# A reordered opening: whole quarters of w_in, an earlier w_out request, two convolution taps on TensorE

## The chip, the cores and the metric

The kernel runs on one core of a Trainium2 chip. The metric is the device time of one execution in microseconds (us), lower is better. A verdict of faster or slower needs 2%, which here is 13.8 us. Each timed execution also gives its span, from the first to the last instruction, which is 1.7 us shorter than its time. A profile is one execution, and its own time is listed with it.

## The reference

A causal convolution over the sequence, with seven softmaxed weights for each of 8 heads, feeds an MLP with the activation h times sigmoid(beta h).

```python
w = exp(weight - max); w = w / (sum(w) + 1e-9)              # (8 heads, 7 taps)
out[b, s, h, g] = sum over k of w[h, k] * x_pad[b, s + k, h, g]
x = out.reshape(32768, 192)
h = x @ w_in                                                # (192, 2048)
g = h * (1 / (1 + exp(-beta * h)))
y = g @ w_out                                               # (2048, 192)
```

x is (8, 4096, 192) in float32.

## The kernel before

The tokens go through in 32 chunks (two times 512 tokens each). A chunk has 16 units `u`, each for 128 of the 2048 hidden columns:

- **TensorE** makes the hidden values of the unit (6 matmuls, two at a time) and, for earlier units, products with w_out ("pairs").
- **ScalarE** applies Silu to the unit: one instruction of 128x1024 elements.
- **VectorE** makes the convolution of a coming chunk: a product and six multiply-adds ("taps"), and other small work.

From chunk 1 on this is a steady pipeline. The change touches the opening only: the loads, chunk 0 (where the convolution of two of three channel groups is made by TensorE with diagonal matrices) and chunk 1's preparation, which is made while chunk 0's 16 units run.

```python
    load_x(x0, 0)                 # chunk 0's tokens, chunk 1's tokens
    load_x(x1, TOK)
    load_w_out(0)                 # four quarters of w_out, SyncE's queue, in this order
    load_w_out(1)
    load(2)                       # chunk 2's tokens
    load_w_out(2)
    load_w_out(3)
    load(3)
    # ... cut ...
    load_w_in(0, FW // 2)         # w_in on GpSimd's queue: first quarter in two halves
    # ... cut ...
    fill(5)                       # filler matmuls on zeros
    # ... cut: product for the softmax weights, filler, casts of x0 ...
    load_w_in(FW // 2, FW)
    for i in range(1, NW):
        load_w_in(i * FW, (i + 1) * FW)
    # ... cut: transposes of chunk 0's tokens with filler between them, the diagonals ...
    new_ct(0)
    for c in range(NG - 1):       # groups 0 and 1 of chunk 0: seven diagonal matmuls each
        pv = in_b() if c else psum_h.tile([128, 2, TOK], FP32, name="ph")
        for k in range(K):
            diag_tap(k, xt0[:, c], pv[:, 0, :])
        for b in range(2):
            cast_rows(nc.scalar.copy, x1b, x1, 2 * c + b)
        nc.scalar.copy(cts[0][:, c, :], pv[:, 0, :])
    # ... cut ...
    for k in range(K):            # group 2 of chunk 0: seven taps on VectorE
        o = HALO - PAD + k
        tap(cts[0][:, NG - 1, :], xt0[:, NG - 1, o : o + TOK].bitcast(FP32), k)
    nc.vector.reciprocal(beta_r, beta)
    scale_w_out(0)                # w_out / beta, one quarter, on VectorE
    # ... cut ...
    CONV1 = {4: (0, 2), 5: (2, 4), 6: (4, K)}   # unit: diagonal taps of chunk 1's group 0
    # ... cut ...
    first_work = {                # VectorE's work in chunk 0, by unit; None is one tap of chunk 1
        4: [None],
        5: [lambda: scale_w_out(1), None],
        7: [None, conv1_evac],    # conv1_evac copies chunk 1's diagonal sums out of PSUM
        8: [None],
        9: [lambda: scale_w_out(2)],
        10: [None, lambda: rows_of(2)],         # casts and transposes of chunk 2
        11: [None],
        12: [lambda: scale_w_out(3), None],
    }
```

In these traces VectorE takes its list in the order of the program: in the kernel before, the scaling of the third w_out quarter waits 0.44 us until 25.05, and the tap behind it starts at 25.93.

Of the kernel before, what the change touches and what calls it, by code (L numbers as in the profile page):

```python
# [17 lines left out]
def kernel(  # L18
# [147 lines left out]

    load_x(x0, 0)
    load_x(x1, TOK)
    load_w_out(0)
    load_w_out(1)  # L170
    load(2)
    load_w_out(2)
    load_w_out(3)
    load(3)

    zeros = setup.tile([128, TOK], BF16)
    nc.vector.memset(zeros, 0.0)
    warm = setup.tile([H, 1], FP32)
    nc.vector.memset(warm, 0.0)  # L179
    nc.scalar.activation(warm, warm, AF.Exp)  # L180

    sel = setup.tile([H, 2, DG], FP32)
# [20 lines left out]
    ident = setup.tile([128, 128], FP32)  # L203
    make_identity(nc, ident)

    def load_w_in(c0, c1):
        for r in range(2):
            nc.gpsimd.dma_start(  # L208
                out=w_in_s[r * DG : (r + 1) * DG, :, c0:c1], in_=w_in_v[:, :, c0:c1]
            )  # L210

    load_w_in(0, FW // 2)

    nmax = setup.tile([H, 1], FP32)
    nc.vector.reduce_max(nmax, cw8, axis=mybir.AxisListType.X, negate=True)
# [38 lines left out]
    nc.tensor.matmul(  # L254
        pw, sel.rearrange("i h p -> i (h p)"), e8, start=True, stop=True
    )
    fill(1, 256)
    nc.tensor.transpose(pb, beta_q, ident[0:NF, 0:NF])
    nc.scalar.copy(beta, pb)
    for b in range(2):  # L260
        cast_rows(nc.vector.tensor_copy, x0b, x0, b)
    nc.vector.reciprocal(rn, pw[:, K : K + 1])
    nc.vector.tensor_scalar_mul(cw, pw[:, 0:K], rn)
    for b in range(2, NB):
        cast_rows(nc.vector.tensor_copy, x0b, x0, b)

    hold = setup.tile([1, 1], BF16)
    nc.gpsimd.tensor_copy(hold, x0b[0:1, 0, 0, 0, 0:1])
    load_w_in(FW // 2, FW)
    for i in range(1, NW):  # L270
        load_w_in(i * FW, (i + 1) * FW)

    diag = setup.tile([128, K, 128], FP32R)
    xt0 = setup.tile([128, NG, HALO + TOK], FP32R)
    nc.vector.memset(xt0[:, :, 0:HALO].bitcast(FP32), 0.0)
    xt1 = setup.tile([128, HALO + TOK], FP32R)
    cts = {}

    def new_ct(s):
        cts[s] = ct_pool.tile([128, NG, TOK], BF16, name="ct")  # L280

    def diag_tap(k, xt, pv, rows=slice(0, 128)):
        o = HALO - PAD + k
        nc.tensor.matmul(  # L284
            pv,
            diag[rows, k, :],
            xt[rows, o : o + TOK],
            start=(k == 0),
            stop=(k == K - 1),
        )  # L290

# [4 lines left out]
    for b in range(NB):  # L296
        pt = pts[b % 2][:, b // 2, 0 : NG * BLK].rearrange("p (c q) -> p c q", c=NG)
        transposes(pt, x0b, b)
        nc.scalar.copy(tokens(xt0, b), pt)  # L299
        fill(1, 256 if b % 2 else 128)  # L300
    fill(1, 256)
    nc.vector.tensor_tensor(
        diag,
        ident.unsqueeze(1).to_broadcast((128, K, 128)),
        cw.unsqueeze(2).to_broadcast((128, K, 128)),
        ALU.mult,
    )

    def scale_w_out(i):
        fcs = slice(i * NQ, (i + 1) * NQ)  # L310
# [9 lines left out]
    for c in range(NG - 1):  # L320
        pv = in_b() if c else psum_h.tile([128, 2, TOK], FP32, name="ph")
        for k in range(K):
            diag_tap(k, xt0[:, c], pv[:, 0, :])
        for b in range(2):
            cast_rows(nc.scalar.copy, x1b, x1, 2 * c + b)
        nc.scalar.copy(cts[0][:, c, :], pv[:, 0, :])

    def tap(dst, src, k):
        scalar = cw[:, k : k + 1]
# [4 lines left out]
                out=dst, in0=src, scalar=scalar, in1=dst, op0=ALU.mult, op1=ALU.add  # L334
            )

    for k in range(K):
        o = HALO - PAD + k
        tap(cts[0][:, NG - 1, :], xt0[:, NG - 1, o : o + TOK].bitcast(FP32), k)
    nc.vector.reciprocal(beta_r, beta)  # L340
    scale_w_out(0)

# [26 lines left out]
        nc.vector.tensor_copy(xt1[:, HALO - PAD :], xt[:, 0, HALO - PAD :])  # L369


    CONV1 = {4: (0, 2), 5: (2, 4), 6: (4, K)}
    conv1_ps = []

    def conv1(u):
# [131 lines left out]
    def rows_of(ch):  # L507
        for h in range(2):
            cast(ch, h)
        xpose(ch)  # L510


    first_work = {
        4: [None],
        5: [lambda: scale_w_out(1), None],
        7: [None, conv1_evac],
        8: [None],
        9: [lambda: scale_w_out(2)],
        10: [None, lambda: rows_of(2)],
        11: [None],  # L520
        12: [lambda: scale_w_out(3), None],
    }

    queue = deque()
    for s in range(N_ST):
        jobs_of(s)
        for u in range(NF):
            if s > 0 or u > 1:
                hidden(s, u)
            elif u == 0:  # L530
                phs = [hidden(0, fc, [0]) for fc in range(2)]
                for j in range(1, NG):
                    for fc in range(2):
                        hidden(0, fc, [j], phs[fc])
                second()
            if s > 0:
                output(s, u, 8 if s < N_ST - 1 else 7, "ab")
            elif u > 7:
                output(s, u, 5, "ab")
            elif u == 3 or u == 7:  # L540
                output(s, u, 5, "a")
            if s == 0:
                if u in CONV1:
                    conv1(u)
                if u == min(CONV1):
                    queue.extend(conv_ops(1, 1))
                for work in first_work.get(u, []):
                    (work or queue.popleft())()
            else:
                if u % 2 and queue:  # L550
                    queue.popleft()()

                if u == 0 and s + 3 < N_CH:
                    load(s + 3)
                if u < 2 and s + 2 < N_CH:
                    cast(s + 2, u)
                if u == 1 and s + 2 < N_CH:
                    xpose(s + 2)
            if u == 12 and s + 2 < N_CH:
                queue.extend(conv_ops(s + 2, 0))  # L560
# [32 lines left out]
```

## Time and profile before

| | before |
|---|---|
| time, median of 4 executions | 692.34 us (692.31 to 693.17) |
| profiled execution | 693.01 us, span 691.3 |
| TensorE busy | 684.0 us |
| first Silu | 14.11 us |
| last tap of chunk 1 ends | 31.73 us |
| first and second Silu of chunk 1 | 32.92 and 34.39 us |

The profile page of the kernel before. The first line is the span; the second is busy time and share of each engine; the third is the DMA queue of w_in (packets, MB, share of time).

```profile
span 691.3 us, 24335 instructions
...
PE 684.0 (99%) x11310; PEld 497.2 (72%) x11310; DVE 527.2 (76%) x466; ACT 579.1 (84%) x531; POOL 8.1 (1%) x20
...
q0 software_dynamic: 2080, 1.57, 1.5%
...
```

TensorE is busy 99%. In the steady state a unit takes 1.307 us (0.65 for the hidden matmuls, 0.65 for eight pairs), and every Silu of 1.11 us is followed by a wait of 0.19 us for TensorE. Nothing in the opening can change that. It can only let it start earlier. Two lines of TensorE's timeline of the kernel before (start, duration, engine and line, operation, count, idle time before it and what ended it):

```profile
...
7.51 3.29 PE L284 MATMUL ph<-xt,diag 128*128 128x512 f32 x7 [0.16 <-ACT xt L299]
10.64 1.79 PE L284 MATMUL pb<-xt,diag 128*128 128x512 f32 x7
...
```

The first seven diagonal matmuls take 3.1 us until the next group starts, the same seven of the next group 1.7 us. Until about 10.6 us these matmuls start 0.43 us apart, then 0.23, and the trace's clock record starts with full clock at 10.60 us. I read the lower clock as half: the record has no entry before 10.60, and the only other value in it is 0.5, at the very end. (The page's clock row shows 9, that is 90% or more, for the whole span all the same.) The Trainium skill, "TensorE: Matmul & The Clock Gate", Part 1, says that full clock is granted after a free-running window of about 3.4 us of activity. The trace agrees with a lower clock first, and with a change in one step (0.43 to 0.23 us within one matmul).

ScalarE's timeline of the kernel before, from the first Silu to the second Silu of chunk 1:

```profile
...
14.11 4.14 ACT L417 ACTIVATE g<-ph,beta 128x1024 bf16<-128x1024 f32 x4 [0.97 <-PE ph L409]
18.96 3.37 ACT L417 ACTIVATE g<-ph,beta 128x1024 bf16<-128x1024 f32 x3 [0.71 <-PE ph L409]
22.57 4.29 ACT L417 ACTIVATE g<-ph,beta 128x1024 bf16<-128x1024 f32 x4 [0.23 <-PE ph L409]
27.34 4.29 ACT L417 ACTIVATE g<-ph,beta 128x1024 bf16<-128x1024 f32 x4 [0.47 <-PE ph L409]
31.86 2.17 ACT L417 ACTIVATE g<-ph,beta 128x1024 bf16<-128x1024 f32 x2 [0.23 <-PE ph L409]
34.39 1.11 ACT L417 ACTIVATE g<-ph,beta 128x1024 bf16<-128x1024 f32 x1 [0.35 <-PE ph L409]
...
```

The 16 Silus of chunk 0 would take 17.2 us in a row. They take 18.8, because ScalarE stands idle 0.71, 0.23, 0.47 and 0.23 us, each time for hidden values that TensorE made late. Why they were late at the end is told by the chain that ended last, in order of time (start, duration, what). It is followed back from the end of the kernel, here from 10 to 36 us:

```profile
...
7.79 17.24 DMA w_out_raw<-in_moe_w_out_dram
...
25.05 0.96 DVE w_out_s L311
26.01 1.20 DVE ct L333
27.20 1.20 DVE xb L106 x2
...
28.48 1.19 DVE ct L333
29.66 0.88 DVE w_out_s L311
...
30.59 0.34 PE pa L442 x4
...
```

The chain starts with a transfer: the third quarter of w_out lands at 25.03 us. VectorE then scales it at once (25.05) and has a fixed queue behind it: a tap, chunk 2's casts, a tap, the fourth quarter, for whose scaling TensorE waits at 30.59.

### The profile page before, as it was taken

How to read it: one execution, taken by the hardware profiler on the slowest of the kernel's cores; microseconds unless marked ns; L12 is line 12 of the kernel's file. 1: busy time of each engine (PE TensorE's matmuls, PEld its weight loads, DVE VectorE, ACT ScalarE, POOL GpSimd, SP SyncE). 2: the span in 40 equal slices, each digit the busy share in tenths (PEclk: the TensorE clock that was granted, in tenths of full speed). 3: DMA queues.
4: the chain of work that ended last, by engine and by line, in shares of the span. 5: the costliest groups of instructions: out<-in, count | busy, mean ns of one | idle time of the engine just before them, and what ended most of it. 6: DMA issues, size and time to landing. Idle time of an engine off the chain costs nothing.

```text
span 691.3 us, 24335 instructions
## 1 busy us (share of the span) xinstructions
PE 684.0 (99%) x11310; PEld 497.2 (72%) x11310; DVE 527.2 (76%) x466; ACT 579.1 (84%) x531; POOL 8.1 (1%) x20
## 2 busy tenths in 40 slices
PE   8999999999999999999999999999999999999997
PEld 5677777777777777777777777777777777777776
DVE  7888877797777797777887777887777977777712
ACT  6888888888888888888888888888888888888893
POOL 4000000000000000000000000000000000000000
PEclk9999999999999999999999999999999999999999
DMA  9754332343332343332444332443323433322111
GB/s 221 169 117 116 90 103 65 92 116 104 99 103 58 104 116 104 93 94 62 113 116 94 102 81 74 116 116 93 102 61 95 116 105 99 102 55 60 48 37 59
DMA packets 121861, 66.86 MB, mean 97 GB/s; under 512 B 53264, under 2 KB 121760, under 8 KB 121760
## 3 DMA queue, kind: packets, MB, share of 16 engines
q1 hardware_dynamic: 119632, 63.73, 34.7%
q0 software_dynamic: 2080, 1.57, 1.5%
q8 instruction: 88, 1.44, 0.9%
q14 instruction: 13, 0.11, 0.1%
q10 hardware_dynamic: 48, 0.01, 0.0%
HBM read 29.89 MB, written 25.17 MB: 80 GB/s over the span
## 4 chain that ended last, share of the span: by engine, by line
PE 95%; DMA 2%; SPq 1%; DVE 1%; ACT 0%; issue 0%
PE ph L409 47%; PE pa L442 24%; PE pb L442 24%; DMA w_out_raw<-in_moe_w_out_dram 2%; SPq L95 1%; DVE ct L333 0%; SPq L160 0%; DVE w_out_s L311 0%; DVE xb L106 0%; ACT g L417 0%; SPq L148 0%; ACT osb L458 0%; DVE xt L121 0%
## 5 line engine op out<-in xcount | busy, mean ns | idle before, releaser
L417 ACT ACTIVATE g<-ph,beta 128x1024 bf16<-128x1024 f32 x512 | 569.7, 1114 | 97.3 <-PE ph L409 91.4
L442 PEld LDWEIGHTS <-g 64*128 64x128 bf16 x8160 | 353.6, 94 | 121.1 <-issue 1.3
L409 PE MATMUL ph<-ct,w_in_s 64*128 64x512 bf16 x3072 | 416.8, 376 | 1.5 <-ACT g L417 0.9
L333 DVE SCALAR_TENSOR_TENSOR ct<-xt,cw,ct 128x1536 bf16<-128x1536 bf16 (+2 forms) x192 | 338.3, 1762 | 2.5
L442 PE MATMUL pa<-w_out_s,g 64*128 64x192 bf16 x4112 | 238.9, 243 | 0.9 <-ACT g L417 0.5
L442 PE MATMUL pb<-w_out_s,g 64*128 64x192 bf16 (+1 forms) x4048 | 224.9, 243 | 0.0
L409 PEld LDWEIGHTS <-w_in_s 64*128 64x128 bf16 x3072 | 143.0, 94 | 64.0 <-DMA w_in_s<-in_moe_w_in_dram 1.6
L460 DVE TENSOR_REDUCE osb<-pa 128x384 f32<-128x768 f32 x64 | 61.3, 958 | 121.5 <-PE pa L442 121.2
L460 DVE TENSOR_REDUCE osb<-pb 128x384 f32<-128x768 f32 x63 | 60.3, 958 | 28.8 <-PE pb L442 28.8
L106 DVE CAST xb<-xf 128x768 bf16<-128x768 f32 x60 | 40.6, 679 | 0.0
L331 DVE TENSOR_SCALAR ct<-xt,cw 128x1536 bf16<-128x1536 bf16 (+2 forms) x32 | 31.2, 974 | 0.2 <-ACT xt L299 0.2
L208 POOL DMA_DIRECT2D w_in_s<-in_moe_w_in_dram x10 | 6.5, 654 | 2.4 <-DMA w_in_s<-in_moe_w_in_dram 2.4
L458 ACT COPY osb<-pb 128x192 f32<-128x192 f32 x1 | 0.3, 319 | 6.7 <-PE pb L442 6.7
L226 PE MATMUL ph<-zeros 128*128 128x512 bf16 (+2 forms) x11 | 4.4, 493 | 1.3 <-DVE warm L179 1.3
L284 PE MATMUL pb<-xt,diag 64*128 64x512 f32 (+1 forms) x21 | 5.1, 445 | 0.0
L121 DVE COPY xt<-xt 128x18 bf16<-128x18 bf16 x27 | 4.3, 160 | 0.0
L311 DVE TENSOR_TENSOR w_out_s<-w_out_raw,beta_r 128x768 bf16<-128x768 f32 x4 | 3.8, 954 | 0.5 <-DMA w_out_raw<-in_moe_w_out_dram 0.4
L284 PEld LDWEIGHTS pb<-xt,diag 64*128 64x128 f32 (+1 forms) x21 | 3.4, 194 | 0.5
L284 PE MATMUL ph<-xt,diag 128*128 128x512 f32 x7 | 3.3, 643 | 0.2 <-ACT xt L299 0.2
L231 ACT CAST x1b<-x 128x384 bf16<-128x384 f32 x4 | 2.7, 717 | 0.7 <-DMA x<-in_x_dram 0.7
L284 PEld LDWEIGHTS ph<-xt,diag 128*128 128x128 f32 x7 | 2.1, 324 | 1.1 <-ACT xt L299 0.6
L226 PEld LDWEIGHTS <-zeros 128*128 128x128 bf16 x11 | 1.4, 140 | 2.1 <-DVE warm L179 1.3
(48 smaller groups left out, 23.2 us busy)
## 6 DMA issues: line engine op xcount, KB each, us to landing
out_dram<-osb SPq DMA_DIRECT2D x127, 192.0 KB, 2.1
xf<-in_x_dram SPq DMA_DIRECT2D x60, 384.0 KB, 4.3
xt<-xb SPq DMA_TRANSPOSE x120, 3.0
x<-in_x_dram SPq DMA_DIRECT2D x4, 384.0 KB, 5.1
w_out_raw<-in_moe_w_out_dram SPq DMA_DIRECT2D x4, 384.0 KB, 13.4
w_in_s<-in_moe_w_in_dram POOLq DMA_DIRECT2D x6, 192.0 KB, 12.2
w_in_s<-in_moe_w_in_dram POOLq DMA_DIRECT2D x4, 96.0 KB, 8.8
out_dram<-osb SPq DMA_DIRECT2D x2, 96.0 KB, 1.6
```

What stands on the lines that cost most here:

```text
L95: nc.sync.dma_start(out=xf[:, h], in_=x_v[p, c * TOK : (c + 1) * TOK, h, :].rearrange("(b q) d -> q b d", q=BLK),)
L106: nc.vector.tensor_copy(xbs[ch][:, :, :, h, :], xfs[ch][:, h].rearrange("q b (p c) -> q b c p", c=NG),)
L121: nc.vector.tensor_copy(dst, last[:, :, HALO + TOK - PAD :])
L208: nc.gpsimd.dma_start(out=w_in_s[r * DG : (r + 1) * DG, :, c0:c1], in_=w_in_v[:, :, c0:c1])
L226: nc.tensor.matmul(pf[:, 0, 0:cols], zeros[:, 0:128], zeros[:, 0:cols], start=True, stop=True)
L284: nc.tensor.matmul(pv, diag[rows, k, :], xt[rows, o : o + TOK], start=(k == 0), stop=(k == K - 1),)
L331: nc.vector.tensor_scalar_mul(dst, src, scalar)
L333: nc.vector.scalar_tensor_tensor(out=dst, in0=src, scalar=scalar, in1=dst, op0=ALU.mult, op1=ALU.add)
L409: nc.tensor.matmul(ph[:, h, :], w_in_s[rows, j, fc * 128 : (fc + 1) * 128], cts[s][rows, j, :], start=(j == 0), stop=(j == NG - 1),)
L417: nc.scalar.activation(gs[s][:, fc], ph, AF.Silu, scale=beta[:, fc : fc + 1])
L442: nc.tensor.matmul(self.po[:, r, b * D : (b + 1) * D], g[rows, fc, self.h, q * BLK : (q + 1) * BLK], w_out_s[rows, fc, :], start=(self.don ...
L460: nc.vector.tensor_reduce(dst, self.po[:, :, 0 : nb * D].rearrange("p r n -> p n r"), axis=mybir.AxisListType.X, op=ALU.add,)
```

## The change

Its intent is to start the steady state earlier. It has five parts: w_in arrives in whole quarters; the third w_out quarter is requested ahead of chunk 2; two of the seven taps of chunk 0's third group go to TensorE; the filler is made longer and some work is moved around it; chunk 1's diagonals are spread over four units, with VectorE's list rearranged.

```diff
     load_x(x0, 0)
     load_x(x1, TOK)
-    load_w_out(0)
-    load_w_out(1)
+    for i in range(NW - 1):
+        load_w_out(i)
     load(2)
-    load_w_out(2)
-    load_w_out(3)
+    load_w_out(NW - 1)
     load(3)
 ...
-    load_w_in(0, FW // 2)
+    load_w_in(0)                      # whole quarters
 ...
-    fill(1, 256)
-    nc.tensor.transpose(pb, beta_q, ident[0:NF, 0:NF])
-    nc.scalar.copy(beta, pb)
+    fill(1, 384)                      # beta's transpose moves behind the tokens' transposes
 ...
-        fill(1, 256 if b % 2 else 128)
+        if b == 0:
+            fill(1, 256)
+        elif b == 1:
+            fill(1, 384)
+    fill(1, 384)
+    nc.tensor.transpose(pb, beta_q, ident[0:NF, 0:NF])
+    nc.scalar.copy(beta, pb)
     fill(1, 256)
 ...
+        nc.scalar.copy(cts[0][:, c, :], pv[:, 0, :])      # now ahead of the x1 casts
         for b in range(2):
             cast_rows(nc.scalar.copy, x1b, x1, 2 * c + b)
-        nc.scalar.copy(cts[0][:, c, :], pv[:, 0, :])
 ...
-    for k in range(K):
+    K_V = 5
+    pv = in_a()[:, 0, :]
+    for k in range(K_V, K):
+        diag_tap(k, xt0[:, NG - 1], pv, k0=K_V)
+    dst = cts[0][:, NG - 1, :]
+    for k in range(K_V):
         o = HALO - PAD + k
-        tap(cts[0][:, NG - 1, :], xt0[:, NG - 1, o : o + TOK].bitcast(FP32), k)
+        tap(dst, xt0[:, NG - 1, o : o + TOK].bitcast(FP32), k)
+    nc.vector.tensor_tensor(dst, pv, dst, ALU.add)
 ...
-    CONV1 = {4: (0, 2), 5: (2, 4), 6: (4, K)}
+    CONV1 = {4: (0, 2), 5: (2, 4), 6: (4, 6), 7: (6, K)}
 ...
-        4: [None],
-        5: [lambda: scale_w_out(1), None],
-        7: [None, conv1_evac],
-        8: [None],
-        9: [lambda: scale_w_out(2)],
-        10: [None, lambda: rows_of(2)],
-        11: [None],
-        12: [lambda: scale_w_out(3), None],
+        4: [None, lambda: scale_w_out(1), None],
+        5: [None],
+        7: [conv1_evac, lambda: scale_w_out(2), lambda: rows_of(2), None],
+        8: [None, lambda: scale_w_out(3)],
+        9: [None],
+        10: [None],
 ...
-                output(s, u, 5, "ab")
-            elif u == 3 or u == 7:
-                output(s, u, 5, "a")
+                output(s, u, 5 if u < NF - 1 else 8, "ab")
+            elif u in QUOTA_A:                            # QUOTA_A = {3: 4, 7: 2}
+                output(s, u, QUOTA_A[u], "a")
```

Cut: the diagonals are built in two instructions instead of one, the four casts of x0 stand together, and the zeros ahead of the first tokens are written earlier.

More of the change, by code (lines that the diff above doesn't have):

```diff
@@ L179 @@
     nc.vector.memset(warm, 0.0)
+    xt0 = setup.tile([128, NG, HALO + TOK], FP32R)
+    nc.vector.memset(xt0[:, :, 0:HALO].bitcast(FP32), 0.0)
     nc.scalar.activation(warm, warm, AF.Exp)
@@ L204, with load_w_in @@
     make_identity(nc, ident)
-    def load_w_in(c0, c1):
+    def load_w_in(i):
+        cols = slice(i * FW, (i + 1) * FW)
         for r in range(2):
             nc.gpsimd.dma_start(
-                out=w_in_s[r * DG : (r + 1) * DG, :, c0:c1], in_=w_in_v[:, :, c0:c1]
+                out=w_in_s[r * DG : (r + 1) * DG, :, cols], in_=w_in_v[:, :, cols]
             )
-    load_w_in(0, FW // 2)
+    load_w_in(0)
     nmax = setup.tile([H, 1], FP32)
@@ L256 @@
     )
-    fill(1, 256)
-    nc.tensor.transpose(pb, beta_q, ident[0:NF, 0:NF])
-    nc.scalar.copy(beta, pb)
-    for b in range(2):
+    fill(1, 384)
+    for b in range(NB):
         cast_rows(nc.vector.tensor_copy, x0b, x0, b)
@@ L263 @@
     nc.vector.tensor_scalar_mul(cw, pw[:, 0:K], rn)
-    for b in range(2, NB):
-        cast_rows(nc.vector.tensor_copy, x0b, x0, b)
     hold = setup.tile([1, 1], BF16)
     nc.gpsimd.tensor_copy(hold, x0b[0:1, 0, 0, 0, 0:1])
-    load_w_in(FW // 2, FW)
     for i in range(1, NW):
-        load_w_in(i * FW, (i + 1) * FW)
+        load_w_in(i)
     diag = setup.tile([128, K, 128], FP32R)
-    xt0 = setup.tile([128, NG, HALO + TOK], FP32R)
-    nc.vector.memset(xt0[:, :, 0:HALO].bitcast(FP32), 0.0)
     xt1 = setup.tile([128, HALO + TOK], FP32R)
@@ L280, in new_ct, with diag_tap @@
         cts[s] = ct_pool.tile([128, NG, TOK], BF16, name="ct")
-    def diag_tap(k, xt, pv, rows=slice(0, 128)):
+    def diag_tap(k, xt, pv, rows=slice(0, 128), k0=0):
         o = HALO - PAD + k
@@ L287, in diag_tap @@
             xt[rows, o : o + TOK],
-            start=(k == 0),
+            start=(k == k0),
             stop=(k == K - 1),
@@ L299 @@
         nc.scalar.copy(tokens(xt0, b), pt)
-        fill(1, 256 if b % 2 else 128)
-    fill(1, 256)
-    nc.vector.tensor_tensor(
-        diag,
-        ident.unsqueeze(1).to_broadcast((128, K, 128)),
-        cw.unsqueeze(2).to_broadcast((128, K, 128)),
-        ALU.mult,
-    )
+        if b == 0:
[5 more added lines that the diff above has]
+    nc.scalar.copy(beta, pb)
+    fill(1, 256)
+    for k0, k1 in ((0, 3), (3, K)):
+        nc.vector.tensor_tensor(
+            diag[:, k0:k1],
+            ident.unsqueeze(1).to_broadcast((128, k1 - k0, 128)),
+            cw[:, k0:k1].unsqueeze(2).to_broadcast((128, k1 - k0, 128)),
+            ALU.mult,
+        )
     def scale_w_out(i):
@@ L513 @@
     first_work = {
-        4: [None],
-        5: [lambda: scale_w_out(1), None],
-        7: [None, conv1_evac],
-        8: [None],
-        9: [lambda: scale_w_out(2)],
-        10: [None, lambda: rows_of(2)],
-        11: [None],
-        12: [lambda: scale_w_out(3), None],
+        4: [None, lambda: scale_w_out(1), None],
[4 more added lines that the diff above has]
+        10: [None],
     }
+    QUOTA_A = {3: 4, 7: 2}
     queue = deque()
```

## The prediction

> **What bounds the kernel now.** TensorE. The page gives PE 684.0 of 691.3 us busy. From 36 us on, the timeline repeats one unit every 1.307 us: six hidden matmul slots (0.65 us) and 16 output matmuls (0.65 us, 0.082 per pair), with ScalarE (1.11 us per unit) waiting 0.19 us for PE each time. 512 units of such work are about 669.6 us (an estimate from these two durations). So only some 22 us of opening and tail are negotiable, and the change touches the first 34 us alone.
>
> **Where the opening loses time (timeline, waits).** First hidden matmul 12.36 us, first Silu 14.11 us; then 16 Silus at a pace of about 1.075 us, which would end at 31.3, but end at 32.9. ScalarE gaps: 0.71 us before unit 4 (second w_in quarter lands at 18.06; PE waits for that DMA), 0.23, 0.47 (third w_out quarter lands at 25.03, scaled until 26.0; PE waits 0.35), 0.23 (fourth w_out quarter scaled late, PE idle 0.41). VectorE finishes chunk 1's convolution at 31.73, after only 1.6 us idle since 14.45 (0.83 us of it waits). The first unit of chunk 1 starts at 32.06.
>
> **What the change does, costed.**
> 1. w_in in whole quarters: 24 of 120 small-load descriptors per DMA engine go. In the packets, the two queues alternate about one for one between 12 and 21 us (65-72 each per half microsecond). The Trainium skill, "DMA: Bandwidth & Descriptors", section "Queues, rings and completion order", states this round robin; the trace agrees. A 96 KB half takes 1.06 us, a 192 KB quarter-half 1.5 us, so quarter 0 lands near 12.1 (its first part now: 11.6), quarter 1 near 15-16.5 instead of 18.06. The 0.71 us gap goes.
> 2. Third w_out quarter ahead of chunk 2: lands near 18.5; the 0.47 us gap goes. Chunk 2's input lands later, near 24, and VectorE reaches its cast near 23.1-23.5: up to 0.5 us of new waiting.
> 3. Two taps on TensorE: VectorE loses two taps of 0.78 us, gains one addition (about 0.6, from a 512-column pass); PE gains two taps (0.25 us each fast, 0.45 slow).
> 4. More filler columns. The first seven diagonal taps run at 0.45 us each, the next seven at 0.245: TensorE is at half clock until 10.6 us. The Trainium skill, "TensorE: Matmul & The Clock Gate", Part 1, gives a free-running busy window of about 3.4 us; denser filler may bring full clock one window earlier (7.2 us). I give this one half. Then the first Silu is bound by w_in, near 13.2; otherwise it stays near 14.1.
> 5. Chunk 1 diagonals over four units: same 1.64 us of PE, evened out against the 1.075 us Silu pace.
>
> **How much is critical.** Before chunk 1, ScalarE could end 1.5-2.4 us earlier, but VectorE has about 16.5 us of queued work from its copies of chunk 1's tokens (start 14.0-14.45), so its convolution cannot end before about 30.9-31.4. That becomes the limit: the first unit of chunk 1 starts near 31.1, about 1.0 us earlier. Everything after shifts by that; one output pair more is left to the end (0.08 us).
>
> **Prediction.** 691.2 us, range 689.8 to 692.4. Faster by over 2%: 1%; within 2%: 98%; slower: 1%.
>
> **Signs.** Right: no PE wait for w_in at unit 4, none for w_out at unit 11; first Silu 13.2-14.1; steady unit unchanged at 1.307; chunk 1's first unit near 31.1, just after VectorE's last tap. Wrong: first Silu later than 14.2 (x1 casts now behind the first copy on ScalarE), or VectorE waiting over 1 us for chunk 2.
>
> **What would make it wrong.** The clock's phase, which could differ by run; the slowest DMA engine delaying landings; VectorE not being the limit, then 2 us or more are won.

## The result, and the profile after

| | before | after |
|---|---|---|
| time, median of 4 executions | 692.34 us (692.31 to 693.17) | 692.68 us (692.25 to 693.48) |
| profiled execution | 693.01, span 691.3 | 692.46, span 690.7 |
| first Silu | 14.11 | 14.31 |
| last tap of chunk 1 ends | 31.73 | 31.87 |
| first and second Silu of chunk 1 | 32.92, 34.39 | 32.57, 33.88 |
| landing of the four w_in quarters (second transfer of each) | 14.90, 18.06, 20.95, 24.74 | 12.00, 14.99, 18.04, 21.14 |
| landing of w_out quarters 1 and 2 | 12.60, 14.77 | 14.36, 18.21 |

The ratio is 1.0003, with a 95% interval from 0.9986 to 1.0021: the same. Ratios are the mean time of one kernel's fast runs over that of the other's of the same rounds, so not quite the ratio of the medians quoted here. A landing is the last of the sixteen completion updates of a transfer in the trace. Of w_in's first quarter, whole at 14.90 before, the half that the first two units need had landed at 11.61.

The page after, the same three lines:

```profile
span 690.7 us, 24335 instructions
...
PE 684.2 (99%) x11311; PEld 518.1 (75%) x11311; DVE 526.6 (76%) x466; ACT 579.1 (84%) x531; POOL 6.8 (1%) x18
...
q0 software_dynamic: 1664, 1.57, 1.4%
...
```

The 416 packets fewer are the smaller w_in requests that are gone. ScalarE's timeline after:

```profile
...
11.38 1.32 ACT L233 CAST x1b<-x 128x384 bf16<-128x384 f32 x2
...
13.08 1.32 ACT L233 CAST x1b<-x 128x384 bf16<-128x384 f32 x2
14.31 16.15 ACT L425 ACTIVATE g<-ph,beta 128x1024 bf16<-128x1024 f32 x15
30.68 1.11 ACT L425 ACTIVATE g<-ph,beta 128x1024 bf16<-128x1024 f32 x1 [0.22 <-PE ph L417]
32.57 1.11 ACT L425 ACTIVATE g<-ph,beta 128x1024 bf16<-128x1024 f32 x1 [0.77 <-PE ph L417]
33.88 1.11 ACT L425 ACTIVATE g<-ph,beta 128x1024 bf16<-128x1024 f32 x1 [0.19 <-PE ph L417]
...
```

The gaps inside chunk 0 are gone: 15 Silus in a row. But a new one of 0.77 us stands before chunk 1's first Silu. The chain that ended last, after, from 22 us on (what comes before it is told below):

```profile
...
22.02 0.28 PE pb L279 x2
...
22.33 0.68 DVE ct L396
...
23.02 0.69 DVE ct L396
...
23.75 0.96 DVE w_out_s L313
24.71 1.20 DVE xb L106 x2
...
25.98 1.20 DVE ct L335
...
27.20 1.28 DVE ct L335
28.49 0.87 DVE w_out_s L313
29.35 1.21 DVE ct L335
...
30.59 1.29 DVE ct L335
...
31.92 0.61 PE ph L417 x4
...
```

The chain no longer starts with a w_out transfer. It comes from TensorE's last diagonal matmul of chunk 1 (22.02, unit 7), goes to VectorE's copy of those sums (22.33), and through VectorE's queue without a gap to the last tap (30.59), for which TensorE's first unit of chunk 1 then waits. Four waits of the changed kernel, from 10 to 35 us (who, for what: us in total, times, longest):

```profile
...
DVE ct L347 <- PE pa L279: 1.8, 1, 1.8
...
DVE w_out_s L313 <- DMA w_out_raw<-in_moe_w_out_dram: 0.6, 1, 0.6
DVE ct L396 <- PE pb L279: 0.6, 1, 0.6
...
PE ph L417 <- DVE ct L335: 0.4, 1, 0.4
...
```

TensorE's diagonal matmuls after, as shown of before:

```profile
...
7.83 3.04 PE L279 MATMUL ph<-xt,diag 128*128 128x512 f32 x7
10.71 1.79 PE L279 MATMUL pb<-xt,diag 128*128 128x512 f32 x7
...
```

The first group is still at half clock for most of its length. This trace has no clock record, but the spacing of the matmuls changes from 0.43 to 0.23 us near 10.4.

**One number carries the rest.** From the second Silu of chunk 1 to the end, the profile of before has 656.89 us and that of after 656.87. In every profile taken later it is 656.86 to 656.89, save one that is told below. So an execution's span says when the second Silu of chunk 1 started: span less 656.88. For the kernel before, fifty further executions were timed beside the experiments and in one of them; their median span is 690.8, so that Silu started at 33.9 us in the middle execution (an estimate by this subtraction). The first profile of before, with 34.39, was one of its slower executions. For the changed kernel nine executions have a median span of 691.2, so 34.3.

### The profile page after: what moved, and what is told of

The parts are those of the page before. It is cut to its first block, busy times and chain, and to the rows that moved or that the text cites. A ratio compares the mean times of both kernels' runs of the same rounds, so it can differ in the third digit from the quotient of the medians.

```text
span 690.7 us, 24335 instructions
## 1 busy us (share of the span) xinstructions
PE 684.2 (99%) x11311; PEld 518.1 (75%) x11311; DVE 526.6 (76%) x466; ACT 579.1 (84%) x531; POOL 6.8 (1%) x18
## 4 chain that ended last, share of the span: by engine, by line
PE 97%; DVE 1%; ACT 1%; issue 0%; ACTq 0%
PE ph L417 47%; PE pa L450 24%; PE pb L450 24%; DVE ct L335 1%; ACT g L425 0%; PE ph L279 0%; ACT x1b L233 0%; DVE w_out_s L313 0%; PE pb L279 0%; PE ph L228 0%; DVE ct L396 0%; DVE xb L106 0%; ACT ct L326 0%; PE pb L240 0%; PE ph L240 0%
## 5 line engine op out<-in xcount | busy, mean ns | idle before, releaser
L450 PEld LDWEIGHTS <-g 64*128 64x128 bf16 x8160 | 367.7, 94 | 106.3 <-ACT g L425 0.7
L417 PE MATMUL ph<-ct,w_in_s 64*128 64x512 bf16 x3072 | 422.8, 376 | 1.3 <-ACT g L425 0.9
L450 PE MATMUL pa<-w_out_s,g 64*128 64x192 bf16 x4112 | 244.2, 243 | 0.6 <-ACT g L425 0.5
L450 PE MATMUL pb<-w_out_s,g 64*128 64x192 bf16 (+1 forms) x4048 | 229.7, 243 | 0.0
L417 PEld LDWEIGHTS <-w_in_s 64*128 64x128 bf16 x3072 | 156.7, 94 | 56.7 <-issue 3.4
L333 DVE TENSOR_SCALAR ct<-xt,cw 128x1536 bf16<-128x1536 bf16 (+2 forms) x32 | 31.1, 972 | 0.0
L233 DVE CAST x0b<-x 128x384 bf16<-128x384 f32 x4 | 1.5, 420 | 2.1 <-DMA x<-in_x_dram 2.1
```

The costliest lines, as they stand in the source:

```text
L333: nc.vector.tensor_scalar_mul(dst, src, scalar)
L417: nc.tensor.matmul(ph[:, h, :], w_in_s[rows, j, fc * 128 : (fc + 1) * 128], cts[s][rows, j, :], start=(j == 0), stop=(j == NG - 1),)
L450: nc.tensor.matmul(self.po[:, r, b * D : (b + 1) * D], g[rows, fc, self.h, q * BLK : (q + 1) * BLK], w_out_s[rows, fc, :], start=(self.don ...
```

## The experiments

Some theories have letters in the expectations. A: VectorE's serial queue is the limit, set late by the landing of w_out. B: TensorE's half clock. C: ScalarE's Silu pace alone. D: the first profile of before was not typical. E: the place of chunk 1's diagonal sums. F: the landing of the third w_out quarter. All kernels here gave correct results. "Run against" means beside executions of the kernel before on the same chip; times are medians of five.

### The changed kernel once more

> The changed kernel itself, once more. Theory A (VectorE's serial chain is the limit): chunk 1's last VectorE tap ends near 31.9 us again and TensorE waits for it in chunk 1's first unit; second Silu of chunk 1 near 33.9; time 692.3 to 693.2, within 0.3 us of the kernel before. Theory C (the difference of 0.3 us in the first timed runs is a loss of its own somewhere after the opening): the Silu of chunk 1 starts earlier than in the kernel before and the span is nevertheless not shorter.

Measured: 692.87 us (692.80 to 693.47) against 692.61 (691.87 to 692.87), ratio 1.0008 (0.9996 to 1.0021). The second Silu of chunk 1 started at 34.19, the last tap ended at 32.19, and TensorE waited for it again. The clock record starts at 10.83 us and the first Silu at 14.78. The changed kernel is 0.3 us slower in the medians both times it was timed beside before; the interval does not exclude zero.

### Scaling the first w_out quarter later

```diff
     nc.vector.reciprocal(beta_r, beta)
-    scale_w_out(0)
 ...
+        scale_w_out(0)                # in second(), behind the copies of chunk 1's tokens
         halo(1, xt0)
```

> The changed kernel, with the scaling of the first w_out quarter moved on VectorE from before to after the copies of chunk 1's tokens. Theory A: the copies no longer wait for the landing of that quarter (14.4 us); they start near 14.5 instead of 15.3, chunk 1's last tap ends near 31.2 instead of 31.9, and the kernel is 0.5 to 0.8 us shorter than the changed kernel. Rival C (ScalarE's Silu pace is the limit): chunk 1's first unit starts at the same time, no gain.

Measured: 692.95 us, no gain: a miss. The copies did start at 14.53 instead of 15.33. But the wait for the diagonal sums grew to 0.73 us and their copy began at 22.41, where it had begun at 22.33. So theory A in this form falls: the wait for w_out was hidden by a later one.

### w_in's first quarter in halves again

```diff
-    load_w_in(0)
+    load_w_in(0, FW // 2)             # and (FW // 2, FW) behind the hold, as before
```

> The changed kernel with w_in's first quarter in two halves again. Theory A, as far as the DMA goes: the first w_out quarter lands near 12.8 to 13.3 again instead of 14.4, VectorE's copies of chunk 1's tokens start up to 0.6 us earlier, but w_in's second quarter lands near 18 and ScalarE's gap before unit 4 (0.7 us) is back. Net within 0.5 us of the changed kernel either way. Rival: if the landing of w_out has another cause (its place in the queue), it stays near 14.4.

Measured: 693.11 us. The first w_out quarter landed at 12.35 instead of 14.36, so its delay was the whole quarters' doing. The profile fell on an execution with full clock only from 12.23 us on: first Silu 15.12, so that nothing could be seen of VectorE's gain, and w_in's second quarter (17.72) came early enough for so late a start. The gap before unit 4 that was expected did not come back. In the six profiles with the filler of the change that have a clock record, full clock comes between 10.36 and 12.47 us.

### All seven taps on VectorE

```diff
-    K_V = 5
-    pv = in_a()[:, 0, :]
-    for k in range(K_V, K):
-        diag_tap(k, xt0[:, NG - 1], pv, k0=K_V)
+    K_V = K
 ...
-    nc.vector.tensor_tensor(dst, pv, dst, ALU.add)
```

> The changed kernel with all seven taps of the third group on VectorE again. VectorE then does 2 x 0.78 us more but loses the addition (0.69) and the wait for TensorE's two taps (1.78 us in the changed kernel). Theory A with the half clock: VectorE is free near 12.75 instead of 13.6, but still waits for w_out at 14.4, so chunk 1's last tap ends at the same 31.9 and the time is the same within 0.3 us; first Silu 0.0 to 0.3 us earlier. Rival (the two taps on TensorE are what ate the gain): faster by 0.5 us or more.

Measured: 692.93 us, first Silu 14.29. The two taps on TensorE neither made nor ate the gain. The profile is of one of its slower executions (693.19; first w_out quarter at 15.07, last tap at 32.60 where 31.9 was expected), so this rests on the times.

### The kernel before once more

> The kernel before, unchanged, for a second profile. In all six profiles so far, the time from the second Silu of chunk 1 to the end is 656.87 to 656.89 us, whichever kernel it was, so a run's span tells when that Silu started. The nine timed runs of before (spans 690.2 to 691.2) then had it at 33.3 to 34.3 us, and the first profile of before (34.39) was one of its slow executions. Theory D (the first profile was not a typical one): this profile shows the second Silu of chunk 1 at 33.5 to 34.1 us, with smaller gaps on ScalarE or earlier landings, and the same 656.88 us after it. If the first profile was typical and the kernel before does better elsewhere, it shows 34.3 or later and a shorter rest.

Measured: 692.48 us (692.05 to 692.87) against 692.49. The profiled execution took 692.76, and its second Silu started at 34.17: a little outside what was expected, and again on the slow side of its own five. The rest was 656.89. With it, a fixed distance shows: VectorE starts scaling the third w_out quarter at 25.05 and 24.83 in the two profiles, and the second Silu follows 9.34 us later in both.

### The copy of the diagonal sums later in VectorE's queue

```diff
-        7: [conv1_evac, lambda: scale_w_out(2), lambda: rows_of(2), None],
+        7: [None, lambda: scale_w_out(2), conv1_evac, lambda: rows_of(2), None],
         8: [None, lambda: scale_w_out(3)],
         9: [None],
-        10: [None],
```

> The changed kernel, with one tap of chunk 1 and the scaling of the third w_out quarter put before the copy of chunk 1's diagonal sums on VectorE, where they stood behind it. Theory E (the spread of chunk 1's diagonals to unit 7 is what holds VectorE: it idles 0.6 to 0.9 us for that copy, and then has 9.5 us of queued work before chunk 1 can start): the idle time goes, chunk 1's last tap ends near 31.3 instead of 31.9, the second Silu of chunk 1 starts near 33.3 to 33.5, and the kernel is 0.4 to 0.7 us shorter than the changed kernel (692.2 to 692.5). Rival C (ScalarE's pace alone): no change.

Measured: 692.96 us: a miss. VectorE's wait went, and the last tap ended at 31.62 in spite of a late clock (12.11). But the first Silu was late with the clock (15.09), and the fourth w_out quarter was now scaled at 29.48 instead of 28.40: TensorE waited 0.5 us for it, ScalarE 0.64 us before unit 15, and the second Silu of chunk 1 started at 34.37.

> The same, and the scaling of the first w_out quarter behind the copies of chunk 1's tokens as in the run scale_late, which alone gained nothing because the time went into the wait for the copy of the diagonal sums. Theory E: now both waits are gone, VectorE runs from 14.5 us without a gap, chunk 1's last tap ends near 31.0, and ScalarE's pace takes over as the limit; second Silu of chunk 1 at 33.1 to 33.3, 0.6 to 0.9 us shorter than the changed kernel. If it equals evac_later, the wait for w_out is off the path in either order.

This adds the later scaling of the first w_out quarter. Measured: 693.67 us against 692.49, ratio 1.0014 (1.0002 to 1.0027): 0.8 us more than the changed kernel where 0.6 to 0.9 less was expected. Its clock came at 12.47, so VectorE's copies began only at 15.54. From there VectorE worked almost without a gap to the scaling of the fourth w_out quarter (29.98), for which TensorE waited 0.5 us and ScalarE, before unit 15, 0.64 us.

### An unbroken filler

```diff
-    fill(5)
+    fill(8)
     pc = in_a()
-    nc.tensor.matmul(pw, sel..., e8, start=True, stop=True)
-    fill(1, 384)
 ...
         transposes(pt, x0b, b)
+        if b == 0:
+            nc.tensor.matmul(pw, sel..., e8, start=True, stop=True)
```

The two small VectorE operations on `pw` move with it.

> The changed kernel with TensorE's first filler lengthened from five to eight matmuls, without a break to 4.7 us, and the small product of the weights moved behind the first transposes. Theory B (half clock): in some executions the full clock comes before 8 us, the seven diagonal taps of the first group take 1.7 us instead of 2.9, the first Silu starts near 13.3 instead of 14.3; but VectorE still holds chunk 1, so the gain is at most 0.6 us (until the wait for the copy of the diagonal sums is the limit: it follows the Silus by 7.6 to 8 us). Rival: the transposes keep TensorE's clock at half whatever stands before them; clock change at 10.4 to 12.3 as in the six profiles, time unchanged.

Measured: 692.61 us (692.54 to 692.69) against 692.49. TensorE's timeline of this kernel:

```profile
...
7.35 1.90 PE L273 MATMUL ph<-xt,diag 128*128 128x512 f32 x7
9.09 1.77 PE L273 MATMUL pb<-xt,diag 128*128 128x512 f32 x7
...
```

Full clock from 4.21 us on, and the first seven taps take 1.7 us. The first Silu starts at 13.60, 0.7 us earlier than in the changed kernel's profile. The second Silu of chunk 1 starts at 33.96, as good as unchanged (33.88). VectorE now waited 2.32 us for the first w_out quarter (landing 14.45), and ScalarE 0.88 us at unit 4, for hidden values that were late because TensorE had waited for VectorE's copies. So the filler can bring the clock forward, the shorter fillers of the change did not, and bringing it forward is worth little with the rest as it is: 692.61 for 692.87, of which 0.12 us is the difference between the two chips' medians of before. Its five times lie within 0.15 us, but those of dense_scale, below, with the same filler, spread over 1.61 us: the filler does not narrow the spread in general.

```diff
 # the kernel before, with the same three edits
```

> The kernel before, with the same unbroken filler (eight matmuls, the small product behind the first transposes). Theory B' (most of the spread from run to run, and the 0.4 us by which the changed kernel is slower in the mean, is the moment at which TensorE gets its full clock, 9.8 to 10.9 us or[...] 12.1 to 12.5): full clock before 8 us, spread of the five times under 0.3 us where the kernel before has 1.7, and 692.0 to 692.4, so at or under fill_dense (692.6). The part of the change that is not clock is then no gain of 1.0 us: it is 0.0 to 0.5 us of loss, through the landing of the first w_out quarter. Rival: with the clock out of the way the change is worth its predicted 1 us, and this kernel takes 693.3 or more.

Measured: 692.67 us (692.48 to 693.05) against 692.54. Full clock from 4.78 us, first Silu 13.67, second Silu of chunk 1 at 34.22, and 9.33 us after the third w_out quarter again (24.89). So the kernel before gains nothing from an early clock. The expected 692.0 to 692.4 was too good, but the rival (693.3) is off by more.

### With the clock out of the way

fill_dense with the later scaling of the first w_out quarter:

> fill_dense, with the scaling of the first w_out quarter behind the copies of chunk 1's tokens. In fill_dense VectorE stood 2.32 us for the landing of that quarter, its copies began at 15.42, and TensorE waited 0.83 us for them, ScalarE 0.88. Theory A (VectorE's chain starts late because that quarter lands 1.8 us later than before): copies begin near 13.9, ScalarE's gap of 0.88 goes, chunk 1's last tap ends near 31.0 to 31.2, and the kernel takes 691.6 to 692.0, 0.6 to 1.0 us less than fill_dense. Rival (that wait is hidden by the later wait for the diagonal sums, as in scale_late): 692.4 to 692.7.

Measured: 692.17 us (691.36 to 692.97) against 692.54, between the two forecasts. The copies began at 14.14, ScalarE's gap was 0.25 instead of 0.88, but the diagonal sums were copied at 22.04 and the last tap ended at 31.57. The copy of the sums no longer waited. VectorE's timeline shows what made it late, the second w_out quarter, which landed at 18.62:

```profile
...
18.65 0.96 DVE L313 TENSOR_TENSOR w_out_s<-w_out_raw,beta_r 128x768 bf16<-128x768 f32 x1 [0.75 <-DMA w_out_raw<-in_moe_w_out_dram]
...
```

The chain that ended last starts with this landing.

The same with the later copy of the diagonal sums:

> The same, and one tap and the scaling of the third w_out quarter ahead of the copy of the diagonal sums. Theory E: with the clock out of the way VectorE runs from 13.9 without a gap, chunk 1's last tap ends near 30.4, then ScalarE's pace is the limit (first Silu 13.6, sixteen at 1.075 to 1.1): second Silu of chunk 1 near 32.3 to 32.8, 691.0 to 691.5 us. If it equals dense_scale, the spread of chunk 1's diagonals cost nothing.

Measured: 692.59 us: a miss. One line of TensorE's timeline shows a new wait:

```profile
...
25.50 0.42 PE L450 MATMUL pb<-w_out_s,g 64*128 64x192 bf16 x6 [0.76 <-DVE ct L396]
...
```

The sums lie in the tile `pb` of PSUM, the memory that TensorE writes its sums to, and the second output job needs that tile at this point. With the copy starting at 24.07, TensorE stood 0.76 us for it, and ScalarE 0.87 us behind that. (In evac_later and evac_scale, with their late clock, TensorE did not wait for this copy.) But the chain that ended last goes another way: from the landing of the second w_out quarter (18.46) through VectorE without a gap to the scaling of the fourth (29.26; 28.10 in dense_scale), for which TensorE then waits 0.5 us. So the order that puts the copy off makes the fourth quarter late, and the wait for `pb` is hidden behind that.

fill_dense with w_in's first quarter in halves:

> fill_dense, with w_in's first quarter in two halves. Theory A: the first w_out quarter lands near 12.4 instead of 14.45, VectorE's copies begin near 13.5 to 13.9, like dense_scale, and the first hidden matmuls wait less for w_in; but its later quarters land up to 0.5 us later at equal load. 691.6 to 692.2. If whole quarters are what makes the gain of the change: 692.8 or more, with ScalarE's gap before unit 2 or unit 4.

Measured: 692.51 us (692.12 to 692.74), between the two forecasts. The first w_out quarter landed at 12.43, but in the profiled execution even the longer filler had full clock only from 9.45 us on, the copies began at 14.63, and the diagonal sums were copied at 22.33 again.

By now eight profiles of kernels with the changed list had the second Silu of chunk 1 at 11.53 to 11.56 us after the start of the copy of the diagonal sums, and that copy 0.42 to 0.46 us after unit 7's Silu started.

### Telling the two pins apart

The changed kernel with the diagonals in three units:

```diff
-    CONV1 = {4: (0, 2), 5: (2, 4), 6: (4, 6), 7: (6, K)}
+    CONV1 = {4: (0, 2), 5: (2, 4), 6: (4, K)}
```

> The changed kernel with chunk 1's diagonals in three units again (4 to 6); everything else as changed. In eight profiles of kernels with the change the second Silu of chunk 1 starts 11.55 us (0.02 either way) after VectorE begins the copy of the diagonal sums, and that copy begins 0.42 to 0.46 us after the Silu of unit 7. Theory E' (that is the new pin: unit 7's diagonals, which follow ScalarE's pace): the copy begins about 0.5 us earlier, when VectorE itself is free (21.7 at the same clock), chunk 1's last tap ends near 31.3, and the time falls by 0.3 to 0.6 us against the changed kernel, to 692.3 to 692.6. Rival (ScalarE's pace): unit 6 grows by 0.23 us on TensorE, a Silu gap of 0.2 returns, no gain.

Measured: 692.40 us (692.16 to 692.78) against 692.65: within the range expected, and 0.5 us under the changed kernel's 692.87 of another chip. Although the first Silu was late (14.83, clock 10.91), the copy of the sums began at 21.86 and the second Silu at 33.70. In the repeat of the changed kernel, with as late a first Silu (14.78), they stood at 22.64 and 34.19. The copy of the sums in VectorE's timeline, first in that repeat, then here:

```profile
...
22.64 1.39 DVE L396 CAST ct<-pb 64x512 bf16<-64x512 f32 x2 [0.94 <-PE pb L279]
...
```

```profile
...
21.86 1.39 DVE L396 CAST ct<-pb 64x512 bf16<-64x512 f32 x2 [0.33 <-PE pb L279]
...
```

Of these 0.78 us, 0.49 reach the second Silu. VectorE waits 0.20 us for chunk 2's input, and the chain that ended last now runs from the first Silu through TensorE alone: VectorE's queue is no longer the limit. The Silu gap that the rival named came back (0.25 us before unit 7), and the kernel gained all the same.

The kernel before with only the request order changed:

```diff
-    load_w_out(0)
-    load_w_out(1)
+    for i in range(NW - 1):
+        load_w_out(i)
     load(2)
-    load_w_out(2)
-    load_w_out(3)
+    load_w_out(NW - 1)
```

> The kernel before, with only the third w_out quarter requested ahead of chunk 2. In three profiles of kernels with the old order, chunk 1's last tap ends 6.67 to 6.68 us after VectorE starts scaling that quarter (24.8 to 25.05, right when it lands) and the second Silu starts 9.33 to 9.34 us after it. Theory F (the landing of that quarter is what pins the kernel before): it lands near 18 to 19, the pin is gone, the second Silu starts 0.4 to 1.0 us earlier; 691.6 to 692.1. Rival (VectorE then waits for chunk 2's input instead, or the landing of w_in at unit 4 pins it): 692.3 to 692.7.

Measured: 692.17 us (691.99 to 692.53) against 692.65 (692.11 to 693.05), ratio 0.9995 (0.9982 to 1.0007), just outside what was expected. ScalarE's timeline of this kernel:

```profile
...
14.28 4.15 ACT L416 ACTIVATE g<-ph,beta 128x1024 bf16<-128x1024 f32 x4 [0.97 <-PE ph L408]
18.66 3.37 ACT L416 ACTIVATE g<-ph,beta 128x1024 bf16<-128x1024 f32 x3 [0.23 <-PE ph L408]
22.27 8.54 ACT L416 ACTIVATE g<-ph,beta 128x1024 bf16<-128x1024 f32 x8 [0.24 <-PE ph L408]
31.04 2.17 ACT L416 ACTIVATE g<-ph,beta 128x1024 bf16<-128x1024 f32 x2 [0.23 <-PE ph L408]
33.57 1.11 ACT L416 ACTIVATE g<-ph,beta 128x1024 bf16<-128x1024 f32 x1 [0.35 <-PE ph L408]
...
```

The gap of 0.47 us is gone, and so is most of the one before unit 4. VectorE reaches the third quarter at 24.23, without waiting for it. The second Silu starts at 33.57, though the first starts later than in the kernel before (14.28 for 14.11). In both profiles of the kernel before, the landing of that quarter was the pin. Both are of slower executions, though, and the interval of the timed gain includes zero.

### What stands behind the pins

All three mended (unbroken filler, later scaling, three units):

> All three causes mended: unbroken filler, the scaling of the first w_out quarter behind chunk 1's copies, diagonals in three units. VectorE runs from 14.0 without a wait for the diagonal sums; chunk 1's last tap ends near 31.0; second Silu near 33.0; 691.4 to 691.9, 0.3 to 0.6 us under dense_scale (692.17). If it equals dense_scale, theory E' fails.

Measured: 692.17 us (691.92 to 692.47) against 692.65, the median of dense_scale, so a miss: theory E' fails for this kernel. The copy of the sums does not wait (21.93), but in dense_scale it did not wait either (22.04). VectorE's timeline has the same wait as there ahead of it:

```profile
...
18.54 0.96 DVE L313 TENSOR_TENSOR w_out_s<-w_out_raw,beta_r 128x768 bf16<-128x768 f32 x1 [0.74 <-DMA w_out_raw<-in_moe_w_out_dram]
...
```

This is the second w_out quarter, which lands at 18.52. Behind it stands chunk 2's input, which lands at 24.91: the chain that ended last starts with it. So three units win only where the sums are what VectorE waits for, as in conv_three.

The same with chunk 2's casts and transposes at the end of VectorE's list:

```diff
-        7: [conv1_evac, lambda: scale_w_out(2), lambda: rows_of(2), None],
+        7: [conv1_evac, lambda: scale_w_out(2), None],
 ...
-        10: [None],
+        10: [None, lambda: rows_of(2)],
```

> The same, with chunk 2's casts and transposes moved behind the last tap of chunk 1 on VectorE (1.43 us of its queue before chunk 1 starts). Theory A/E' (VectorE's queue is the limit): the last tap ends near 29.7, then ScalarE's pace is the limit (its sixteenth Silu near 30.3), second Silu of chunk 1 near 32.6 to 32.9, 691.1 to 691.5 us. Rival: chunk 2's transposes come too late for its own taps and chunk 2 or 3 pays; then the rest after the second Silu is longer than 656.9 us.

Measured: 692.47 us against 692.65. The second Silu of chunk 1 started at 32.94, the earliest of all profiles and next to the expected 32.6 to 32.9, though the last tap ended at 30.43 and not at 29.7. Then the rest took 658.04 us instead of 656.88, as the rival had it. Two waits of this kernel, from 33 to 75 us:

```profile
...
DVE ct L333 <- DMA xt<-xb: 4.2, 1, 4.2
...
PE ph L417 <- DVE ct L335: 1.0, 1, 1.0
...
```

VectorE waits 4.2 us for chunk 2's transposes, and chunk 2's first unit is late for it: 0.65 us won at chunk 1 (against dense_scale_three), 1.16 lost at chunk 2.

The last two runs ask whether the named pins are all. First the unbroken filler, halves of w_in's first quarter and three units; the request order and the two taps of the change stay:

> The changed kernel with unbroken filler, w_in's first quarter in halves and diagonals in three units: the parts of the change that set a new wait are taken back, the request order and the two taps on TensorE stay. If the account is whole (pins: landing of the first and second w_out quarter through whole quarters of w_in, diagonal sums through the fourth unit, clock), VectorE runs from about 14.0 to 14.6 without a wait over 0.2 us, chunk 1's last tap ends near 30.9 to 31.2, the second Silu starts at 32.9 to 33.3, 691.5 to 691.9 us. If it stays at 692.2 or more, a further limit is there that I have not named.

Measured: 692.08 us (692.02 to 692.37) against 692.47, between the two forecasts. In the profiled execution, the slowest of the five, the copies began at 13.79 and neither w_out quarter cost VectorE more than 0.6 us. But w_in's second quarter landed at 18.26, as in the kernel before. One line of TensorE's timeline:

```profile
...
18.30 0.60 PE L418 MATMUL ph<-ct,w_in_s 64*128 64x512 bf16 x4 [0.77 <-DMA w_in_s<-in_moe_w_in_dram]
...
```

TensorE waits at unit 4 for w_in, and the chain that ended last runs from this landing through TensorE alone to the second Silu (33.78). The diagonals of units 4 to 6 move with it, and VectorE waits 2.06 us for their sums, off that chain. So this limit was there too, and the account before this run was not whole: the whole quarters do serve unit 4 when the first units start early enough (in the profile before, the gap there was 0.71 us).

Second, the kernel before with request order and unbroken filler:

> The kernel before with the request order changed and unbroken filler. First Silu near 13.7; the wait for w_in's second quarter (landing near 18) is then the pin at unit 4: a ScalarE gap of 0.3 to 0.9 us there, the second Silu of chunk 1 at 33.2 to 33.6, 691.8 to 692.2: no better than before_w_out (692.17). If the clock were the limit of the kernel before, it gains the 0.5 us of the earlier first Silu and takes 691.7 or less.

Measured: 691.97 us (691.42 to 692.64) against 692.47, ratio 0.9992 (0.9978 to 1.0005): the time is in the expected range. In the profiled execution, again the slowest, ScalarE's gap at unit 4 was 0.89 us and the second Silu started at 34.05, later than expected. This is the lowest median, 0.5 us under the kernel before on the same chip, and under both medians of the changed kernel (692.68 and 692.87). Its interval does not exclude that it equals the kernel before.

## Why the prediction was right or wrong

The class (within 2%) was right. The size was not: 691.2 us (689.8 to 692.4) was forecast and 692.68 measured.

1. **Right: what the changed loads do for w_in and for the third w_out quarter.** w_in's first quarter was put at 12.1 us and landed at 12.00; the second at 15 to 16.5, and landed at 14.99. ScalarE's gaps of 0.71 and 0.47 us went. (The third w_out quarter's landing is not in the trace; VectorE scaled it at 23.75 without a wait.) VectorE did not wait for chunk 2 in this profile (up to 0.5 us was feared; conv_three shows 0.20).
2. **Wrong: the step "VectorE has about 16.5 us of queued work from its copies of chunk 1's tokens (start 14.0-14.45), so its convolution cannot end before about 30.9-31.4. That becomes the limit: the first unit of chunk 1 starts near 31.1, about 1.0 us earlier."** VectorE was the limit, but its queue was neither started so early nor free of waits. It ended at 31.87, and the first unit of chunk 1 went on at 31.92 (32.06 before). From the start of the copies to the last tap it took 16.54 us, as forecast, but 0.61 of them were a wait.
   - The start was 15.33: the first w_out quarter landed at 14.36 instead of 12.60, because w_in's larger packets share the DMA engines with it: from 9.5 to 12.5 us w_in's queue moved 211 KB before and 369 after, and SyncE's queue, which carries w_out and the tokens, 597 and 305. The prediction costed what whole quarters do for w_in and not what they take from w_out. The run w_in_half (12.35) shows it.
   - In the middle of the queue stands the copy of chunk 1's diagonal sums. The change had moved the last of them to unit 7, so that they follow the Silus: copy at 22.33 after a wait of 0.61 us, last tap 9.54 us later, in fixed distance. (Before, VectorE waited 1.18 us for these sums, until 21.90, but the third w_out quarter hid that.) The prediction called the four units "evened out" and gave them no cost. conv_three shows it: with three units the copy comes 0.8 us earlier at the same first Silu. Where the copy did not wait (dense_scale), three units changed nothing (dense_scale_three).
   - The first of these did not count by itself (scale_late: no gain), because the second wait followed. That is why single repairs gained little. With the early clock it counted: the second Silu at 33.57 in dense_scale for 33.96 in fill_dense.
3. **Wrong: the base of the subtraction.** The gain was read from the profile of one execution of 693.01 us and taken off the median of 692.34. Measured by the two profiles, the change won 0.55 us (693.01 to 692.46). But the middle execution of before has its second Silu near 33.9, not 34.39, so even the full 1.0 us taken from the profile would have led only to 692.0. The miss of 1.48 us is 0.67 from this base, 0.37 from the gain in the profiles (0.55 for 1.0 less 0.08), 0.22 because the changed kernel's own profiled execution was that much below its median, and 0.22 because the prediction went to the good side of its own sum (692.34 - 1.0 + 0.08 is 691.42).
4. **The clock: half a chance was given, and it was the wrong half.** In no profile with the filler of the change did full clock come before 9.8 us; it came between 10.4 and 12.5, as it came at 10.60 and 9.83 before. (Two of these eight traces have no clock record; there the spacing of the matmuls shows it, near 10.4.) With the longer, unbroken filler it came at 4.05 to 5.91 in eight of nine profiles (9.45 in the other). Even then the time fell by 0.1 to 0.3 us in the changed kernel and not at all in before: the step from an earlier first Silu to an earlier chunk 1 fails, since w_out's landing holds VectorE (until 14.55 in fill_dense, 24.89 in before_dense).
5. **The two taps on TensorE** cost what was said (0.25 us each, addition 0.69 for 0.6). At half clock VectorE waits 1.8 us for them, which the prediction had not. It is hidden; taps_seven moves nothing.
6. **The stated sign "x1 casts now behind the first copy on ScalarE"** is in the profile: the casts at 11.38 and 13.08 end at 14.4, and the first Silu starts at 14.31, on the chain. No run moves them alone, but the traces give a size: after, the first unit's last hidden matmul ends at 14.13 and its Silu starts 0.18 us later, behind the casts; before, it starts 0.09 us after that matmul (14.02). So the casts hold the first Silu by about 0.1 us (an estimate from these two).

What stays open: why the kernel before spreads over 1.8 us from run to run (spans 690.1 to 691.9). In its two profiles the landing of the third w_out quarter sets the second Silu, and before_w_out spreads over 0.54 us, but no fast execution of before was caught in a profile, so that this landing makes the spread is not shown. The gap of 0.3 us between the medians of before and after is within the intervals, and is not explained further than by points 2 and 4.

## What to carry to other kernels

While the DMA engines are full, a transfer that is made earlier or larger makes another one later (here w_out's first quarter by 1.8 us): cost the loads that lose, and find the first instruction in program order that waits for each. A queue that is served in order has more than one wait in it, so read the fixed distances between events over several profiles (here 9.34, 9.54 and 656.88 us) to see which wait counts, and expect the next one close behind: conv_three, which takes one away, won 0.49 us at the second Silu. Then ask the chain that ended last, not the longest wait: in dense_evac_scale and dense_half_three the wait that stood out was off it. Before a gain of 0.1% is subtracted from a median, check that the profile it was read from is an execution near that median.

## What the Trainium skill lacked or had wrong

- "TensorE: Matmul & The Clock Gate", Part 1, gives the length of the window (about 3.4 us sustained) but not how busy it has to be. Here, five filler matmuls from 1.26 us and then filler and transposes with gaps never brought full clock before 9.8 us (eleven profiles); with eight filler matmuls in a row from 1.26 us it came at 4.05 to 5.91 in eight of nine profiles. In two of the eleven the spacing of the matmuls shows it and not a clock record.
- The same page, Part 4, says that transposes do not count as busy in the same way. That would fit: twelve of them stand between 4.8 and 6.9 us, and full clock came at 9.83 or later. No run separates transposes from gaps.
- The same page, Part 1, says that the moment of the change varies from run to run, by 0.5 us either way. That it varies agrees, but over the kernels here that share a filler it varies by more: 10.4 to 12.5 us for the filler of the change, and 4.05 to 9.45 for the longer one.
- "DMA: Bandwidth & Descriptors", "Queues, rings and completion order", states the round robin at packet granularity. It does not say what share of bytes that gives. (A packet of the page holds several descriptors; the trace counts pieces of 1024 or 768 bytes as packets, and does not show which of the two alternates.) In both traces, from 15 to 19 us, the queues of w_in and of w_out move 64 to 73 packets each per half microsecond, packets of 1024 and 768 bytes, so the larger packet takes the larger share (about 64 against 51 KB), and larger w_in packets delayed w_out's first two quarters by 1.8 and 3.4 us.
